# The key-value blocks of linear attention as four 32-column matmuls each instead of one 128-column matmul

## The chip, the cores and the metric

The kernel runs on one core of a Trainium2 chip. The metric is the device time of one execution in microseconds (us), taken as the median over several runs; one further execution is profiled, and every row shown here comes from that one.

## What is computed

The reference normalises x, runs linear attention over it, and multiplies the result with a gated feed-forward layer. The part that matters here is the state of the attention, `kv`: 32 heads, each with a 32x32 matrix.

```python
H = 32; Dh = D // H                      # D = 1024, S = 2048
phi = lambda t: jnp.where(t > 0, t + 1, jnp.exp(t)) + 1e-6
pq, pk = phi(q), phi(k)
kv = jnp.einsum("bhsd,bhse->bhde", pk, v)    # 32x32 for each head
z = jnp.einsum("bhsd->bhd", pk)
num = jnp.einsum("bhqd,bhde->bhqe", pq, kv)
den = jnp.einsum("bhqd,bhd->bhq", pq, z)[..., None] + 1e-6
...
xn = _layernorm(x, axis=-1)
s = A(xn)                                # (num / den) @ wo
g = _silu((_silu(xn @ w1) * (xn @ w3)) @ w2)
return x + s * g
```

## The kernel before

All large products are written as seven-product schemes on 2x2 blocks (names such as `B11`, `T2`, `S1`, `c22` are their operands and sums). Each single product is done by `mm3`: three matmuls of 128x512 on rounded high and low parts (lines 103, 104, 105). The order in which TensorE gets its work is the order in which the program is written; a scheduler places the instructions of the other engines.

The sequence tokens are handled in two halves. The second half projects keys and queries, then forms g, the product of the transposed normalised rows with the keys (`row_products`, `g_d`), so that kv can be had from g and the value columns of `wqkv` without forming v. After that the loop over 14 column pairs of w1 and w3 runs (`gemm`, names `ag`, `bg`, `cg`, `dg` for the gate and `au`, `bu`, `cu`, `du` for the up projection), and the rest of the attention is fed into it as small jobs: after each of the seven products, `catch_up` takes the next step of a queue of jobs (`attention_work`, `go_on`).

Two jobs matter here. `key_values(j)` makes the state of four heads (128 columns of D): its two steps, e = 0 and 1, each load a tile `gw` (four 128x128 blocks of g and four of the value weights) and accumulate four matmuls into one 128x128 part of a PSUM bank `kv`. There are eight j, so 16 steps in all, which I call kv blocks. These matmuls have plain float32 operands, and the trace shows two weight loads and two matmuls for each of them. Off the four 32x32 squares of the diagonal the 128x128 result mixes different heads, so after e = 1 VectorE multiplies it with `hmask` (one on the four squares, zero elsewhere) and writes `kvf`. `merge_wo` splits `kvf` into `kvm` and multiplies it with rows of wo (`wos`), giving `wp`.

Two older places in the kernel already put 32-column matmuls at separate column positions: `spread_z` (line 816, tile `zc`: eight matmuls of 128x32 weights with two columns streamed) and `denominators` (line 852, tile `den`: four matmuls at a time, 256 columns streamed).

Of the kernel before, what the change touches and what calls it, by code (L numbers as in the profile page):

```python
# [16 lines left out]
P = 128  # L17
# [5 lines left out]
def tile_linear_attention_times_swiglu(  # L23
# [10 lines left out]
    nc = tc.nc  # L34
# [3 lines left out]
    ND = D // P  # L38
# [5 lines left out]
    DH = D // H  # L44
# [6 lines left out]
    def bank(name):  # L51
        return ps.tile([P, C], F32, tag="bank", name=name)
# [5 lines left out]
    hmask = const.tile([P, P], F32, name="hmask")  # L58
# [64 lines left out]
    def job_tile(shape, name):  # L123
        return praw.tile(shape, F32, tag="job", bufs=4, name=name)
# [771 lines left out]
    kvf = {}  # L896

    def key_values(j):

        acc = []  # L900

        def load(e):
            t = job_tile([P, 2, ND // 2, P], f"gw{j}_{e}")
            nc.sync.dma_start(out=t[:, 0], in_=g_d[2 * e + j % 2][:, :, j // 2 * P:(j // 2 + 1) * P])
            rows = wqkv[e * C:(e + 1) * C, 2 * D + j * P:2 * D + (j + 1) * P]
            nc.sync.dma_start(out=t[:, 1], in_=rows.rearrange("(k p) n -> p k n", p=P))
            return t

        def steps(e, t):
            if not acc:  # L910
                acc.append(bank(f"kv{j}")[:, :P])
            for k in range(ND // 2):
                nc.tensor.matmul(acc[0], lhsT=t[:, 1, k], rhs=t[:, 0, k], start=e + k == 0, stop=bool(e) and k == ND // 2 - 1)
            if e:
                kvf[j] = st.tile([P, P], F32, tag="kvf", bufs=1, name=f"kvf{j}")
                nc.vector.tensor_mul(kvf[j], acc[0], hmask)
            yield True

        return [Job(lambda e=e: load(e), lambda t, e=e: steps(e, t)) for e in range(2)]
# [237 lines left out]
    def second_weights(i, n, k):  # L1157
        if (i, n, k) not in asked:
            ask(i, n, k, small)
        return asked[i, n, k]  # L1160
# [109 lines left out]
    def layer_place(n, i, k):  # L1270
        return (pw[0] if k else pw0).tile([P, 2, C], FR, tag=f"{n}_{k}", name=f"{n}_{k}")

    acc = []
    layers = [Segment(f"B{i}", (f1 - f0) // 2, i == 0, i == len(FB) - 1, layer_place,
                      lambda n, _, k, i=i: second_weights(i, n, k),
# [41 lines left out]
```

## Time and profile before

| | |
|---|---|
| median of 3 runs | 2343.28 us (2342.56 to 2346.6) |
| the profiled execution | 2346.91 us, of which the span is 2345.1 us |
| TensorE matmul busy | 2300.3 us, 98% of the span |
| VectorE, ScalarE, GpSimd busy | 1780.5, 923.9, 687.0 us |
| granted TensorE clock | 0.995 of full speed |
| kv matmuls (line 913) | 128 records of 274 ns mean, between 1162 and 1342 us |

In the views of the profile PE is TensorE's matmul side and PEld its weight load; DVE is VectorE, ACT ScalarE, POOL GpSimd. Matmuls are pipelined, so that a record lasts longer than the step from one start to the next. A timeline row with "x8" merges eight records: its length goes from the first start to the last end.

### The profile page before, as it was taken

Reading aid. Unit: us, or ns where it says so; the run is one execution under the profiler, and the core shown is the slowest. Engines: PE = TensorE matmul, PEld = TensorE weight load, DVE = VectorE, ACT = ScalarE, POOL = GpSimd, SP = SyncE. Lnnn points to the kernel's source line nnn. Section 1 sums busy time; section 2 is a strip of 40 time slices with the busy share of each in tenths; the row PEclk is TensorE's granted clock in tenths of the full one; section 3 lists DMA queues with packets and bytes.
Section 4 is the critical chain, followed back from the end, with each engine's and each line's share of the span. In section 5 each row is a group of like instructions: output and inputs, shape, how many; then the busy total and the mean of one; then the engine's idle time right before and its main releaser. Section 6 shows DMA issues by size and latency. Waiting matters only on the chain.

```text
span 2345.1 us, 30980 instructions
## 1 busy us (share of the span) xinstructions
PE 2300.3 (98%) x10368; PEld 1888.9 (81%) x10368; DVE 1780.5 (76%) x2830; ACT 923.9 (39%) x1639; POOL 687.0 (29%) x854
## 2 busy tenths in 40 slices
PE   6999999999999999999999999999999999999998
PEld 5788878888887888777888888888887888888876
DVE  8887888888877776557867688887755666767798
ACT  5555343433232554433243332334323634242433
POOL 5220333376766221001423434342310000000033
PEclk9999999999999999999999999999999999999999
DMA  6555455576668645786666666665756565665688
GB/s 234 179 184 179 153 184 184 169 227 215 215 218 314 224 146 191 257 257 204 211 188 187 193 195 216 195 217 166 242 173 193 171 191 178 219 211 182 189 267 265
DMA packets 353695, 479.69 MB, mean 205 GB/s; under 512 B 24208, under 2 KB 262800, under 8 KB 353424
## 3 DMA queue, kind: packets, MB, share of 16 engines
q1 hardware_dynamic: 315808, 357.63, 48.5%
q0 software_dynamic: 37728, 120.09, 15.8%
q8 instruction: 81, 1.33, 0.2%
q14 instruction: 78, 0.64, 0.1%
HBM read 306.71 MB, written 174.59 MB: 205 GB/s over the span
## 4 chain that ended last, share of the span: by engine, by line
PE 70%; DVE 5%; DMA 3%; issue 1%; ACT 1%; SPq 0%; DVEq 0%; ACTq 0%
PE g L103 2%; PE g L104 2%; PE g L105 2%; PE aB L105 1%; PE dB L103 1%; PE aB L103 1%; PE aB L104 1%; PE cB L105 1%; PE dB L104 1%; PE dB L105 1%; PE cB L104 1%; PE cB L103 1%; DMA rS4B<-h_d 1%; PE bB L103 1%; PE bB L104 1%
## 5 line engine op out<-in xcount | busy, mean ns | idle before, releaser
L751 POOL DMA_DIRECT2D h_d<-sg x112 | 82.8, 740 | 253.8 <-DVE sg L747 163.1
L1065 POOL DMA_DIRECT2D u_d<-uB x32 | 17.3, 541 | 403.4 <-DVE uB L1048 361.0
L96 DVE TENSOR_TENSOR xy<-xy,xy 128x512 fp32r<-128x512 f32 x112 | 73.0, 686 | 65.3 <-ACT xy L95 65.2
L95 ACT CAST xy<-xy 128x512 fp32r<-128x512 f32 x112 | 65.1, 620 | 102.5 <-PE g L105 56.8
L104 PE MATMUL g<-xy,xy 128*128 128x512 f32 x224 | 87.7, 391 | 1.0 <-DVE xy L96 1.0
L105 PE MATMUL g<-xy,xy 128*128 128x512 f32 x224 | 87.1, 390 | 0.0
L103 PE MATMUL g<-xy,xy 128*128 128x512 f32 x224 | 82.6, 398 | 0.0
L518 POOL DMA_DIRECT2D y_d<-y x48 | 34.6, 722 | 139.7 <-ACT y L538 79.8
L1048 DVE TENSOR_TENSOR acc<-cB,acc 128x512 f32<-128x512 f32 x50 | 34.4, 687 | 41.2 <-PE cB L105 41.2
L1048 DVE TENSOR_TENSOR acc<-dB,acc 128x512 f32<-128x512 f32 x56 | 38.5, 688 | 30.0 <-PE dB L105 29.8
L731 POOL TENSOR_TENSOR hs<-hs,sg 128x256 f32<-128x256 f32 x56 | 60.6, 1082 | 0.1
L733 POOL TENSOR_TENSOR hs<-sg 128x256 f32<-128x256 f32 x56 | 56.8, 1014 | 0.0
L103 PEld LDWEIGHTS g<-xy,xy 128*128 128x128 f32 x224 | 41.8, 187 | 14.1 <-issue 3.7
L889 POOL DMA_DIRECT2D qs_d<-qd x32 | 18.1, 565 | 117.4 <-DVE qd L885 80.1
L1179 POOL DMA_DIRECT2D s_d<-s x32 | 17.3, 541 | 117.6 <-DVE s L1048 69.7
L104 PEld LDWEIGHTS g<-xy,xy 128*128 128x128 f32 x224 | 42.1, 188 | 10.8 <-DVE xy L96 1.7
L734 POOL TENSOR_TENSOR hs<-sg,hs 128x256 f32<-128x256 f32 x56 | 49.9, 891 | 1.5
L730 POOL TENSOR_TENSOR hs<-sg,sg 128x256 f32<-128x256 f32 x56 | 50.0, 893 | 1.2
L766 POOL TENSOR_TENSOR w<-w 128x256 f32<-128x256 f32 x28 | 27.3, 975 | 78.5 <-DMA w<-in_B_w 78.3
L105 PEld LDWEIGHTS g<-xy,xy 128*128 128x128 f32 x224 | 42.1, 188 | 8.9
L759 POOL DMA_DIRECT2D h_d<-hs x60 | 45.8, 765 | 3.5 <-POOL hs L734 2.4
L95 ACT CAST XS4B<-rS4B 128x384 fp32r<-128x384 f32 (+1 forms) x40 | 19.7, 493 | 60.8 <-PE cB L105 41.1
(5315 smaller groups left out, 8316.8 us busy)
## 6 DMA issues: line engine op xcount, KB each, us to landing
h_d<-hs POOLq DMA_DIRECT2D x60, 256.0 KB, 3.5
h_d<-sg POOLq DMA_DIRECT2D x56, 256.0 KB, 3.8
w<-in_B_w SPq DMA_DIRECT2D x56, 256.0 KB
wt_d<-w SPq DMA_DIRECT2D x28, 512.0 KB
xy<-x_d SPq DMA_DIRECT2D x28, 512.0 KB
xy<-y_d SPq DMA_DIRECT2D x28, 512.0 KB
h_d<-hs SPq DMA_DIRECT2D x52, 256.0 KB
y_d<-y POOLq DMA_DIRECT2D x48, 256.0 KB, 3.0
```

Of the source, the lines that this page charges most:

```text
L95: nc.scalar.copy(out=hi, in_=src)
L96: return nc.vector.tensor_sub(out=lo, in0=src, in1=hi.bitcast(F32))
L103: nc.tensor.matmul(acc, lhsT=wh, rhs=ah, start=start, stop=False, skip_group_check=True)
L104: nc.tensor.matmul(acc, lhsT=wh, rhs=al, start=False, stop=False, skip_group_check=True)
L105: return nc.tensor.matmul(acc, lhsT=wl, rhs=ah, start=False, stop=stop, skip_group_check=True)
L730: e.tensor_add(out=s1, in0=a21, in1=a22)
L731: e.tensor_sub(out=s2, in0=s1, in1=a11)
L733: e.tensor_sub(out=s3, in0=a11, in1=a21)
L734: e.tensor_sub(out=s4, in0=a12, in1=s2)
L751: nc.gpsimd.dma_start(out=h_d[i][2 * h + c][:, 2 * n:4 * n + 2, k], in_=src)
L759: queue.dma_start(out=h_d[i][2 * h + c][:, 6 + 4 * e:10 + 4 * e, k], in_=o[e].rearrange("p (e s) -> p e s", s=P))
L1048: return V.tensor_add(out=c, in0=src, in1=c)
```

## The change

Each float32 matmul of 128x128 in `key_values` becomes four: for each of the four heads g the 128x32 slice of the value weights is the stationary operand on columns 32g to 32g+31 of TensorE, the matching 128x32 slice of g is streamed, and the 32x32 result goes to partitions 32g to 32g+31 of the PSUM tile, which is now 32 columns wide. So 256 matmuls stand where 64 stood. The multiplication with the mask reads the 32 columns four times, by a broadcast, and writes the same 128x128 `kvf`.

```diff
         def steps(e, t):
             if not acc:
-                acc.append(bank(f"kv{j}")[:, :P])
+                acc.append(bank(f"kv{j}")[:, :DH])
             for k in range(ND // 2):
-                nc.tensor.matmul(acc[0], lhsT=t[:, 1, k], rhs=t[:, 0, k], start=e + k == 0, stop=bool(e) and k == ND // 2 - 1)
+                for g in range(P // DH):
+                    c = slice(g * DH, (g + 1) * DH)
+                    nc.tensor.matmul(acc[0][c], lhsT=t[:, 1, k, c], rhs=t[:, 0, k, c], skip_group_check=True,
+                                     start=e + k == 0, stop=bool(e) and k == ND // 2 - 1, tile_position=(0, g * DH))
             if e:
                 kvf[j] = st.tile([P, P], F32, tag="kvf", bufs=1, name=f"kvf{j}")
-                nc.vector.tensor_mul(kvf[j], acc[0], hmask)
+                heads = [P, P // DH, DH]
+                nc.vector.tensor_mul(kvf[j].rearrange("p (g c) -> p g c", c=DH),
+                                     acc[0].unsqueeze(1).to_broadcast(heads), hmask.rearrange("p (g c) -> p g c", c=DH))
             yield True
```

On TensorE, at the first kv block, between the first product of a gate projection (`ag`) and its second (`bg`), the order before is:

```order
L104 MATMUL ag_2__9770<-A_1_6432,B11g_2__9702 128x512
L105 MATMUL ag_2__9770<-A_1_6432,B11g_2__9702 128x512
L913 MATMUL kv_9789<-gw_0_9618 128x128 x4
L103 MATMUL bg_2__9794<-S_1_6433,T2g_2__9766 128x512
L104 MATMUL bg_2__9794<-S_1_6433,T2g_2__9766 128x512
```

and after it (the numbers at the ends of names are counters and shift with the added instructions):

```order
L104 MATMUL ag_2__9770<-A_1_6432,B11g_2__9702 128x512
L105 MATMUL ag_2__9770<-A_1_6432,B11g_2__9702 128x512
L915 MATMUL kv_9789<-gw_0_9618 32x32 x16
L103 MATMUL bg_2__9806<-S_1_6433,T2g_2__9766 128x512
L104 MATMUL bg_2__9806<-S_1_6433,T2g_2__9766 128x512
```

Sixteen matmuls stand where four stood, at the same place; this is so at all 16 kv blocks, and nothing else moves on TensorE.

On VectorE, after the second kv block, where the mask is applied (`kvf`), `B11u` is an operand of the next up projection. Before:

```order
L464 TENSOR_TENSOR ug_2__9769<-bg_2__9794,ug_2__9769 128x512
L96 TENSOR_TENSOR B11u_2__9886<-wu_2__9700,B11u_2__9886 128x512
L916 TENSOR_TENSOR kvf_9820<-kv_9789,hmask 128x128
L347 TENSOR_TENSOR wu_2__9700<-wu_2__9700 128x4x128 x2
L471 TENSOR_TENSOR c22g_2__9834<-cg_2__9795,ug_2__9769 128x512
L96 TENSOR_TENSOR kvm_9843<-kvf_9820,kvm_9843 128x128
```

and after:

```order
L464 TENSOR_TENSOR ug_2__9769<-bg_2__9806,ug_2__9769 128x512
L920 TENSOR_TENSOR kvf_9844<-kv_9789,hmask 128x128
L96 TENSOR_TENSOR B11u_2__9910<-wu_2__9700,B11u_2__9910 128x512
L347 TENSOR_TENSOR wu_2__9700<-wu_2__9700 128x4x128 x2
L471 TENSOR_TENSOR c22g_2__9858<-cg_2__9807,ug_2__9769 128x512
L96 TENSOR_TENSOR kvm_9867<-kvf_9844,kvm_9867 128x128
```

The mask moves ahead of one neighbour. Such moves, by one or two places, are found at seven of the eight masks, and at two of them `kvm` moves ahead of a subtraction of line 347 as well. Besides, one subtraction of GpSimd (line 734) and one DMA issue of SyncE (line 759) move by a few places; ScalarE's order is the same.

## The prediction

> **What bounds the kernel now.** I read the page first, then the busy time by stages, then the chain of waits in the stage of the kv blocks, and last the timeline around single blocks.
>
> ```profile
> span 2345.1 us, 30980 instructions
> PE 2300.3 (98%) x10368; PEld 1888.9 (81%) x10368; DVE 1780.5 (76%) x2830; ACT 923.9 (39%) x1639; POOL 687.0 (29%) x854
> ```
>
> TensorE is busy for 98% of the span. Whether it is the bound in the stage of the change, and afterwards, is seen in the stretches from 1156 us (just before the first kv block) to 1345 us (just after the last), and from there to the end:
>
> ```profile
> 1156.00:1345.00 189.00, 189.00 (x897) 158.40 (x896) 133.29 (x188) 66.93 (x122) 68.59 (x74) 1.00 0.61 189
> 1345.00:1640.00 295.00, 295.00 (x1302) 244.19 (x1302) 244.70 (x409) 101.99 (x173) 114.67 (x136) 1.00 0.64 199
> 1640.00:2345.00 705.00, 691.51 (x3036) 568.39 (x3034) 493.18 (x837) 266.73 (x514) 84.62 (x119) 1.00 0.67 207
> ```
>
> The first number is the length, the second PE's busy time, the fourth DVE's (133 of 189 us in the first row), the one after the counts the granted clock. In the first two stretches PE has no gap at all; in the last it lacks 13.5 of 705 us. So what is taken from PE between 1156 and 1345 us should come off the end, unless something that PE nearly waits for becomes late. The chain of waits in the window from 1150 to 1350 us agrees:
>
> ```profile
> by line: PE kv L913 7.1%; PE wp L103 1.6%; PE wp L105 1.6%; PE wp L104 1.6%; PE du__10685 L104 0.9%; PE du__10685 L105 0.9%; PE cu__11035 L103 0.9%; PE du__10685 L103 0.9%; PE dg__10872 L105 0.9%; PE cg__9795 L103 0.9%; PE cu__9966 L103 0.9
> 1162.45 0.89 PE kv L913 x8
> ...
> 1175.14 0.23 PE wp L103
> ...
> 1341.13 0.89 PE kv L913 x8
> ```
>
> All of it is PE work, and the kv blocks are 7.1% of 200 us, 14.2 us, in sixteen pieces of 0.89 us. This is the most that the change could ever win: 0.6% of the time.
>
> **The change part by part.** What a block costs now is read around the first one, on PE:
>
> ```profile
> 1161.61 0.39 PE L103 MATMUL ag__9770<-A,B11g__9702 128*128 128x512 f32 x1
> 1161.83 0.39 PE L104 MATMUL ag__9770<-A,B11g__9702 128*128 128x512 f32 x1
> 1162.06 0.39 PE L105 MATMUL ag__9770<-A,B11g__9702 128*128 128x512 f32 x1
> 1162.29 1.05 PE L913 MATMUL kv<-gw 128*128 128x128 f32 x8
> 1163.10 0.48 PE L103 MATMUL bg__9794<-S,T2g__9766 128*128 128x512 f32 x1
> 1163.41 0.40 PE L104 MATMUL bg__9794<-S,T2g__9766 128*128 128x512 f32 x1
> ```
>
> Without a block, a 512-column matmul starts 0.227 us after the one before (1161.61, 1161.83, 1162.06). From 1162.06 to 1163.41 there are 1.35 us with two such steps in them, 0.45 us, so the block costs 0.90 us; it is the same for all 16, since the chain shows 0.89 at the first and the last. Inside it the eight records (two for each of the four float32 matmuls) step by (1.05 - 0.275)/8 = 0.10 to 0.11 us, 0.275 us being the length of one.
>
> The new block is not in this trace, but its form is. Tile `zc` has matmuls of plain float32 with 128x32 weights on rotating column positions, like the new ones, only with two columns streamed instead of 32, and eight matmuls (16 records) instead of 16 (32 records). Around it:
>
> ```profile
> 924.34 0.22 PEld L816 LDWEIGHTS zc<-eps,zb 128*32 128x32 f32 x16 [0.35 <-issue]
> ...
> 924.03 0.39 PE L105 MATMUL g<-xy,xy 128*128 128x512 f32 x1
> 924.35 0.31 PE L816 MATMUL zc<-eps,zb 128*32 128x2 f32 x16
> 924.58 0.50 PE L103 MATMUL g<-xy,xy 128*128 128x512 f32 x1
> 924.92 0.40 PE L104 MATMUL g<-xy,xy 128*128 128x512 f32 x1
> 925.15 0.39 PE L105 MATMUL g<-xy,xy 128*128 128x512 f32 x1
> ```
>
> Three things are to be seen. The weight loads do not start under the matmul before, as they do in the old block, but after 0.35 us in which the profile shows nothing to wait for: entering the 32-column form costs a drain, and leaving it another, as the 0.34 us step after 924.58 shows. Still, from 924.03 to 924.92 are only 0.89 us, 0.44 us above two normal steps. And the 16 records run four at a time. The timeline cut off later and later in this block shows how it grows:
>
> ```profile
> 924.35 0.21 PE L816 MATMUL zc<-eps,zb 128*32 128x2 f32 x4
> ...
> 924.35 0.24 PE L816 MATMUL zc<-eps,zb 128*32 128x2 f32 x8
> ...
> 924.35 0.28 PE L816 MATMUL zc<-eps,zb 128*32 128x2 f32 x12
> ```
>
> Each further group of four, one for each column position, adds 0.03 us (0.21, 0.24, 0.28, 0.31). Does streaming more columns break this? Tile `den` streams 256 at each of the four positions:
>
> ```profile
> 926.53 0.39 PE L105 MATMUL g<-xy,xy 128*128 128x512 f32 x1
> 926.85 0.64 PE L852 MATMUL den<-pqd,zb 128*32 128x256 f32 x8
> 927.41 0.50 PE L103 MATMUL g<-xy,xy 128*128 128x512 f32 x1
> 927.75 0.39 PE L104 MATMUL g<-xy,xy 128*128 128x512 f32 x1
> ...
> 926.85 0.42 PE L852 MATMUL den<-pqd,zb 128*32 128x256 f32 x4
> ```
>
> The second group of four adds 0.64 - 0.42 = 0.22 us, so a column costs about 0.22/256 = 0.86 ns for all four positions together, and 32 columns 27 ns. That is just under the 0.03 us step of `zc`, which must then be set by the loading of 32 weight columns, and loading and streaming overlap (the old block shows it too: loads and matmuls of 0.19 and 0.275 us in steps of 0.11). So I take 0.032 us for each group of four, that is for both streaming and loading.
>
> The new block has 32 records, eight groups of four. Its cost is that of `zc`, 0.45 us (0.44 by the step at 924.92, a few hundredths more by the slower steps just behind), plus four more groups at 0.032, 0.13 us, plus 0.03 us for the 30 columns by which its last group streams longer: 0.61 us. The check with `den`: two groups fewer than `zc`, -0.06, and 254 more columns in each of two, +0.43 less the 0.03 that the load had cost, gives 0.79; measured from 926.53 to 927.75 it is 0.77. So the block goes from 0.90 to 0.61 us, and 16 of them save 16 x 0.29 = 4.7 us (4.2 to 5.2 for 0.02 us of uncertainty in each block and the read-off).
>
> VectorE's mask now reads 32 PSUM columns four times:
>
> ```profile
> 1166.81 0.69 DVE L96 TENSOR_TENSOR B11u__9886<-wu__9700,B11u__9886 128x512 fp32r<-128x512 f32 x1
> ...
> L916 DVE TENSOR_TENSOR kvf<-kv,hmask x8: 282/283/292, 1167.4 to 1342.5; 128x128 f32<-128x128 f32 x8
> L96 DVE TENSOR_TENSOR kvm<-kvf,kvm x8: 281/283/293, 1170.3 to 1345.4; 128x128 fp32r<-128x128 f32 x8
> ```
>
> It makes as many elements, so I take the same 283 ns; a broadcast read could at worst double it, 2.3 us over all eight. Either way it is hidden: DVE is free for 56 of the 189 us, and from the first `kvf` (1167.4 us) on `kvm` comes at 1170.3 and `wp` on PE only at 1175.14 us (in the chain above). The moves of this mask by one or two neighbours, of 283 ns against 0.69 us, have the same cover; without it PE would wait by at most that, 0.7 us at a block. Loads, their sizes and their issue places are unchanged. The new matmuls' only waits are those for the loads at the head of each block, as before.
>
> What is late next? Nothing in the stage, where PE has no gap at all; later PE waits 13.5 us in total, which a 4.7 us earlier arrival could lengthen a little. I take nothing off for it. The profiled execution of 2346.91 us (2345.1 span) would be 2342.2; against the median of 2343.28 us the forecast is **2338.6 us**. The change is 0.20%, and 0.2% (4.7 us) is about what a measurement of this kernel can tell from no change, so the forecast lies on the edge between faster and the same.
>
> **The rivals.** *The groups of four run one after another.* `zc` streams two columns, and its weights are loaded once for each position; in the new block each position has other streamed data. If every record took its own 0.032 us, the 32 of them would take 1.02 us where I count 0.26, the block 1.37, and the time would rise by 16 x 0.47 = 7.5 us to **2350.8**. Against it stands `den`, where four positions with other data each stream 256 columns in the time of one. The Trainium skill, "TensorE: Matmul & The Clock Gate", section "Wait — 56ns, not 53.3ns?", says that matmuls never start closer than about 25 ns to each other however few columns they stream. By that 32 records would take 0.8 us and the time would rise by about 4 us, an estimate from that page; the trace disagrees, since the 16 records of `zc`, of 0.17 us each, lie within 0.31 us, 9 ns apart. I give 0.11 to this rival.
>
> *TensorE's sequencer cannot feed the blocks*, the rival that ends slower by most. How far it runs ahead is seen from its waits for the loads:
>
> ```profile
> L913 PEld LDWEIGHTS kv<-gw x128: 187/192/192, 1162.1 to 1341.6; 128*128 128x128 f32 x128
> L913 PEldq EVENT_SEMAPHORE  x16: 51/51/51, 1158.2 to 1337.6; - x16
> ```
>
> The first wait passes at 1158.2, 3.9 us before the first load starts: 17 steps of 0.227 us, about 34 instructions. `zc` has 32 in all, so it may have stood in that queue as a whole; the new block has 64, of which some 30 must come while it runs. The old block proves only 0.055 us for each (a load and a matmul in 0.11). At that the 30 need 1.65 us, the block costs 2.0 us, and the time rises by 16 x 1.1 = 17.6 us to **2361**. It decides from 18 ns an instruction on, where the block is back at 0.90 us. The same page and section give 62 ns for a matmul whenever the sequencer decodes in software, which by my estimate from it would make the time rise by about 7 us. One place in the trace speaks against both, at the start of the kernel, in the window from 36.85 to 37.1 us and the timeline behind it:
>
> ```profile
> L165 PEldq EVENT_SEMAPHORE  x2: 51/51/51, 36.9 to 37.0; - x2
> ...
> 37.35 0.60 PE L165 MATMUL tS<-ident,xb 128*128 128x128 f32 x4
> 37.79 0.60 PE L165 MATMUL tS<-ident,S1x 128*128 128x128 f32 x4
> 38.23 0.60 PE L165 MATMUL tA<-ident,xb 128*128 128x128 f32 x4
> 38.66 0.33 PE L165 MATMUL tS<-ident,xa 128*128 128x128 f32 x1
> ```
>
> Of these groups of transposes the first and the last need two engines each, and so a wait of the sequencer's own. Between the two waits it issued the first three groups, 24 instructions, in less than 0.15 us: 6 ns each or less. I give this rival 0.08.
>
> *What is gained in the stage is lost behind it.* The longest of PE's waits after 1345 us is this:
>
> ```profile
> PE cB L103 <- DVE acc L1048: 1.0, 1, 1.0
> ```
>
> VectorE is not hurried by an earlier PE, and the DMA engines are busy for 67% of the last stretch; were the whole gain to end in such a wait, the time would stay at **2343.3**. Against it: the longest wait is 1.0 us and came once, and 1345 to 1640 us has none. I give it 0.13.
>
> **How the numbers follow.** My forecast has 0.68. Of that, 0.47 goes to a gain over 0.2% and 0.21 to one just below, since its own range of 2337 to 2340.5 us (4.2 to 5.2 us saved, and the scatter of medians) is cut in the middle, and a stretch that is all PE leaves little that could eat into it. With the lost gain the chance of "same" is 0.34; the two rivals that slow it down hold 0.19. The range of 2336.5 to 2346 us takes in the forecast and the lost gain, up to near the highest of the runs shown (2346.6), and leaves out the two slower rivals.
>
> **What would show it.** In the changed profile PE should have 512 records of the new kv line instead of 128, so 10752 in all; a block should show the idle time of some 0.35 us before its first load, its 32 records should lie within 0.46 us (0.26 from first to last start), and the step from the 512-column matmul before it to the second one behind should be 1.06 instead of 1.35 us. From 1156 us to the end of the last block it should take 4.7 us less, without PE waiting for `kvf`, `kvm` or `wos`. The mask should stay near 283 ns. Records of a block spread evenly over 1 us mean that the positions run in turn; a burst of half of them and then a trickle means the sequencer; blocks as forecast with longer waits after 1640 us mean the lost gain.

## The result and the profile after

The changed kernel takes 2338.3 us (median of 15 runs, 2336.32 to 2342.83), the one before in the same comparison 2344.15 us; the ratio is 0.9979, with a 95% interval from 0.9972 to 0.9986. That is 5.85 us or 0.2% less: a small gain, but the interval lies wholly below 1. The forecast was 2338.6 us. The profiled execution took 2340.79 us.

The page of the changed kernel, PE's stretches from before the first block to behind the last and from 1635 us to the end (length, then PE's busy time), and the chain of waits from 1150 to 1350 us:

```profile
span 2339.0 us, 31747 instructions
PE 2296.4 (98%) x10752; PEld 1880.5 (80%) x10752; DVE 1778.8 (76%) x2830; ACT 926.3 (40%) x1639; POOL 691.1 (30%) x854
...
1155.50:1345.50 190.00, 190.00 (x1306) 153.10 (x1306) 138.67 (x196) 69.27 (x126) 68.89 (x73) 1.00 0.65 197
...
1635.00:2339.00 704.00, 691.06 (x3035) 568.38 (x3033) 492.37 (x836) 267.29 (x514) 85.93 (x119) 1.00 0.67 207
...
1161.84 0.39 PE kv L915 x32
1162.22 0.43 PE bg__9806 L103
...
1336.12 0.39 PE kv L915 x32
```

PE is as full as before. A kv block is 0.39 us in the chain where it was 0.89, but the matmul behind it has 0.43 us in the chain where a normal step is 0.23, so part of the price of leaving the 32-column form is counted there. So I compare from the first to the last block: 1162.45 to 1341.13 is 178.68 us before, 1161.84 to 1336.12 is 174.28 us now. Fifteen blocks lie between, and 4.40/15 = 0.293 us each, 4.7 us for sixteen. The spans differ by 6.1 us; the other 1.4 us are spread over the time before 1160 us (0.6 us, where the two programs are the same) and after the stage (0.8 us), which I take for the scatter of single executions.

The first block in the timeline of PE, with the weight loads first, and the same block cut off at two earlier points:

```profile
1161.76 0.35 PEld L915 LDWEIGHTS kv<-gw 128*32 128x32 f32 x32 [0.35 <-issue]
...
1161.45 0.39 PE L105 MATMUL ag__9770<-A,B11g__9702 128*128 128x512 f32 x1
1161.77 0.46 PE L915 MATMUL kv<-gw 128*32 128x32 f32 x32
1162.15 0.50 PE L103 MATMUL bg__9806<-S,T2g__9766 128*128 128x512 f32 x1
1162.49 0.39 PE L104 MATMUL bg__9806<-S,T2g__9766 128*128 128x512 f32 x1
...
1161.77 0.24 PE L915 MATMUL kv<-gw 128*32 128x32 f32 x4
1161.77 0.36 PE L915 MATMUL kv<-gw 128*32 128x32 f32 x19
```

Before its first load the weight-load side stands idle for 0.35 us, for which the profile names no releaser. The 32 records lie within 0.46 us, and from 1161.45 to 1162.49 are 1.04 us, 0.59 above two normal steps.

### The profile page after: what moved, and what is told of

It reads as the page before. It is cut to its first block, busy times and chain, and to the rows that moved or that the text cites. A ratio compares the mean times of both kernels' runs of the same rounds, so it can differ in the third digit from the quotient of the medians.

```text
span 2339.0 us, 31747 instructions
## 1 busy us (share of the span) xinstructions
PE 2296.4 (98%) x10752; PEld 1880.5 (80%) x10752; DVE 1778.8 (76%) x2830; ACT 926.3 (40%) x1639; POOL 691.1 (30%) x854
## 4 chain that ended last, share of the span: by engine, by line
PE 69%; DVE 6%; issue 5%; DMA 5%; ACT 1%; POOL 0%; SPq 0%; DVEq 0%; ACTq 0%; POOLq 0%
PE g L103 2%; PE g L104 2%; PE g L105 2%; PE cB L103 1%; PE cB L105 1%; PE cB L104 1%; PE dB L105 1%; PE dB L103 1%; PE dB L104 1%; PE aB L105 1%; PE aB L103 1%; PE aB L104 1%; PE bB L105 1%; PE bB L103 1%; PE bB L104 1%
```

## The experiments

The theory is the one of the forecast: a block costs about 0.33 us for entering and leaving the 32-column form and some 0.032 us for every group of four records, one at each column position. Below, the cost of a block is read as before, from the last 512-column matmul ahead of it to the second behind it, less two steps of 0.227 us. Experiments with one run are read from their traces alone, since single times scatter by several us. The diffs show the lines that matter, against the changed kernel.

### The change again, twice

No edit; two more comparisons of the changed kernel.

> The changed kernel once more, beside the next three on one chip. The theory (a kv block costs 0.61 us instead of 0.90 us, sixteen times, all of it on TensorE and none given back): 4.7 us below the kernel before, ratio 0.998. The rival that the 6 us of the first comparison hold another gain besides the blocks: 6 us or more below again.

> The changed kernel a third time, on another chip, to narrow its ratio: 4.7 us from the blocks less what a stray wait takes, 0.998 to 0.9985.

Measured: ratios 0.9988 (0.9979 to 0.9997) and 0.9980 (0.9972 to 0.9989), medians 2339.37 against 2343.18 us and 2339.5 against 2343.4 us, so 3.8 and 3.9 us less than before. Both profiled executions show one wait of PE in the stage, the same in both, which the profile of the kernel before and the first one of the changed kernel do not have:

```profile
PE dg__10607 L103 <- DVE c22g__10641 L477: 0.6, 1, 0.6
```

The blocks cost what they cost in the first profile. In these executions 0.6 of the 4.7 us is given back, because VectorE has not yet read the PSUM bank that the next product writes (line 477). Of the VectorE operations ahead of it, the one on `T1u` (line 96) took 1.78 us in both, against 0.68 us in the first profile of the changed kernel; why is open. In the profile of the kernel before it took 1.78 us too, without a wait of PE. Both comparisons come out below 4.7 us, which speaks against another gain besides the blocks. Their intervals reach from 0.7 to 4.9 and from 2.6 to 6.6 us, so the first of the two excludes a gain of 6 us and the second alone would not.

### All 128 columns streamed at each position, with the old mask

```diff
-                acc.append(bank(f"kv{j}")[:, :DH])
+                acc.append(bank(f"kv{j}")[:, :P])
...
-                    nc.tensor.matmul(acc[0][c], lhsT=t[:, 1, k, c], rhs=t[:, 0, k, c], skip_group_check=True,
+                    nc.tensor.matmul(acc[0][c], lhsT=t[:, 1, k, c], rhs=t[:, 0, k], skip_group_check=True,
...
+                nc.vector.tensor_mul(kvf[j], acc[0], hmask)
```

> Still 32 weight columns at four positions, but each position streams all 128 columns of g, and the mask is the old one over 128x128. Theory (the gain comes from streaming a quarter of the columns at each position, side by side): each group of four takes 0.11 us instead of 0.033, first to last start of a block 0.80 instead of 0.26 us, the block costs 1.23 us; 10 us above the changed kernel and 5 us above the one before. Rival one (the gain comes from the mask reading 32 columns, or from the moved VectorE order): as slow as before, 0.0 to 0.5 us off. Rival two (it comes from four positions as such): as fast as the changed kernel.

Measured: 2351.04 us, ratio 1.0034 (1.0021 to 1.0047), 7.9 us above the kernel before. The first block on PE:

```profile
1161.54 0.39 PE L105 MATMUL ag__9770<-A,B11g__9702 128*128 128x512 f32 x1
1161.86 1.08 PE L915 MATMUL kv<-gw 128*32 128x128 f32 x32
1162.87 0.50 PE L103 MATMUL bg__9806<-S,T2g__9766 128*128 128x512 f32 x1
1163.21 0.40 PE L104 MATMUL bg__9806<-S,T2g__9766 128*128 128x512 f32 x1
```

From 1161.54 to 1163.21 are 1.67 us, 1.22 above two steps; I had expected 1.23. The 0.32 us more than in the old block make 5.1 us for sixteen, which is also what the spans of the two profiled executions differ by (2350.2 against 2345.1 us); the 7.9 us of the medians have an interval from 4.9 to 11.0 us. So neither rival fits: the time is not that of the kernel before, nor that of the changed one. Four positions as such are a loss here, since eight groups at 0.11 us take as long as the eight records of the old block and the drain comes on top. The gain of the change is that each position streams a quarter of the columns while the other three do the same.

### Both steps in one block, in the new form and in the old

The first tile is kept at e = 0, and all matmuls are issued at e = 1:

```diff
-            for k in range(ND // 2):
-                for g in range(P // DH):
-                    c = slice(g * DH, (g + 1) * DH)
-                    nc.tensor.matmul(acc[0][c], lhsT=t[:, 1, k, c], rhs=t[:, 0, k, c], skip_group_check=True,
...
             if e:
+                for i in range(ND):
+                    k = i % (ND // 2)
+                    for g in range(P // DH):
+                        c = slice(g * DH, (g + 1) * DH)
+                        u = both[i // (ND // 2)]
+                        nc.tensor.matmul(acc[0][c], lhsT=u[:, 1, k, c], rhs=u[:, 0, k, c], skip_group_check=True,
+                                         start=i == 0, stop=i == ND - 1, tile_position=(0, g * DH))
```

> Both steps of a column group in one block: nothing is done at e = 0, and at e = 1 all eight pieces of the contraction, 64 matmuls, 128 records. Theory (of the 0.61 us of a block 0.35 are entering and leaving the 32-column form, 0.033 a group): eight entries fewer, 16 groups in each block, 0.88 us for it instead of twice 0.61, 2.7 us below the changed kernel. Rival (TensorE's sequencer can feed only what stands in its queue of some 33 instructions; 64 went well because half of them stood there): the second half of a block comes slower than 0.033 us a group, and the gain shrinks or turns. Rival two (the first tile is held longer, the loads behind it come late): a wait of TensorE for gw.

> The version with both steps in one block again, beside the changed kernel. Theory: eight drains of 0.33 us fewer, 2.6 us below the changed kernel, ratio to the kernel before 0.9969 to 0.9975. Rival (its lead over the changed kernel was scatter): within 1 us of it.

The control does the same to the kernel before: `nc.tensor.matmul(acc[0], lhsT=u[:, 1, k], rhs=u[:, 0, k], start=i == 0, stop=i == ND - 1)` over all eight i at e = 1, with the old mask.

> The control for the one with 64 matmuls in a block: the kernel before, with both steps in one block of eight 128x128 matmuls. Theory (the old form has no drain at its entry, and at its exit only some 0.1 us): 0.1 us less for each pair, 0.8 us in total, the same as before within the interval. Rival (putting the steps together is itself the gain, by fewer interruptions of the projections): 2 us or more below the kernel before.

Measured in the new form: 2335.63 and 2337.25 us, ratios 0.9972 (0.9963 to 0.9982) and 0.9969 (0.9958 to 0.9980), so 3.7 and 2.3 us below the changed kernel beside it. In the old form: 2343.7 us, ratio 1.0003 (0.9995 to 1.0012). The block of the new form, and of the old:

```profile
1165.86 0.39 PE L105 MATMUL bg__9789<-S,T2g__9766 128*128 128x512 f32 x1
1166.18 0.76 PE L920 MATMUL kv<-gw 128*32 128x32 f32 x64
1166.87 0.51 PE L103 MATMUL cg__9790<-S,T3g__9731 128*128 128x512 f32 x1
1167.21 0.39 PE L104 MATMUL cg__9790<-S,T3g__9731 128*128 128x512 f32 x1
```

```profile
1161.72 0.39 PE L105 MATMUL bg__9789<-S,T2g__9766 128*128 128x512 f32 x1
1161.95 1.95 PE L917 MATMUL kv<-gw 128*128 128x128 f32 x16
1163.65 0.48 PE L103 MATMUL cg__9790<-S,T3g__9731 128*128 128x512 f32 x1
1163.96 0.40 PE L104 MATMUL cg__9790<-S,T3g__9731 128*128 128x512 f32 x1
```

In the new form the joint block costs 1.35 - 0.45 = 0.90 us where two of the changed kernel cost 1.2; in the old form it costs 1.79 us, as much as two of 0.90. Joining steps is worth something only where a block has a switch of form to save. The saving of 0.3 us for each pair is close to the third of a microsecond that I take for the price of switching; the next experiment shows what the difference is. The old form lost not even the 0.1 us that I had expected of it. PE never waits for `gw` although the first tile is held longer. In the second profile of the joint form PE waits 0.9 us at the place where the changed kernel waited 0.6. This version is faster than the kernel before in both comparisons. Against the changed kernel the intervals of the ratios overlap in both, so its lead there rests on the blocks: 0.3 us less for each of eight pairs, 2.4 us.

### The same matmuls twice

```diff
-            for k in range(ND // 2):
+            for i in range(ND):
+                k = i % (ND // 2)
```

> Each block does its 16 matmuls twice over (kv is doubled by it; the work is what counts). Theory: eight more groups of four at 0.033 us, a block at 0.88 us instead of 0.61, 4.2 us above the changed kernel, just below the kernel before; first to last start 0.53 us. Rival (the feed of TensorE's queue): the groups beyond the queue come slower, above 0.6 us from first to last start.

Measured (kv comes out doubled; the time alone is of interest): 2343.35 us, ratio 1.0001 (0.9992 to 1.0011). The first block, and cut off earlier and earlier:

```profile
1160.75 0.39 PE L105 MATMUL ag__9770<-A,B11g__9702 128*128 128x512 f32 x1
1161.07 0.76 PE L916 MATMUL kv<-gw 128*32 128x32 f32 x64
1161.76 0.51 PE L103 MATMUL bg__9822<-S,T2g__9766 128*128 128x512 f32 x1
1162.10 0.39 PE L104 MATMUL bg__9822<-S,T2g__9766 128*128 128x512 f32 x1
...
1161.07 0.61 PE L916 MATMUL kv<-gw 128*32 128x32 f32 x48
1161.07 0.52 PE L916 MATMUL kv<-gw 128*32 128x32 f32 x36
1161.07 0.46 PE L916 MATMUL kv<-gw 128*32 128x32 f32 x32
```

A block costs 0.90 us, 0.02 more than expected. The first eight groups end at 0.46 us, 0.03 us apart; the ninth ends 0.06 us later, the next three 0.03 us apart, and the last four take 0.15 us together. So the second half is some 0.05 us longer than eight steps of 0.03 us, and the joint block of the experiment before has the same length (0.76 us for 64 records): without this loss, joining two blocks would have saved the third of a microsecond. A feed as slow as the forecast's rival needs is excluded: the rival decides from 18 ns an instruction on, and beyond the 34 or so instructions that stand ready, over 90 more came in about 0.57 us, 6 ns each at most. What causes the loss in the second half stays open; that a feed of some 4 ns an instruction has a part in it is not excluded.

### Two heads at a time on 64 columns

```diff
-                for g in range(P // DH):
-                    c = slice(g * DH, (g + 1) * DH)
+                for g in range(2):
+                    c = slice(g * 2 * DH, (g + 1) * 2 * DH)
```

> Two heads at a time: 64 weight columns at two positions, 64 columns streamed, the mask reading 64 columns twice. Theory (steps go with the columns loaded and streamed): eight groups of two at 0.058 us, 0.43 us from first to last start, a block at about 0.82 us. Rival (the drain at entry and exit is longer or shorter with the number of positions): the same steps, but another fixed part than 0.35 us.

One run, 2342.64 us. The first block:

```profile
1160.70 0.39 PE L105 MATMUL ag__9770<-A,B11g__9702 128*128 128x512 f32 x1
1161.02 0.69 PE L915 MATMUL kv<-gw 128*64 128x64 f32 x16
1161.63 0.50 PE L103 MATMUL bg__9798<-S,T2g__9766 128*128 128x512 f32 x1
1161.96 0.39 PE L104 MATMUL bg__9798<-S,T2g__9766 128*128 128x512 f32 x1
```

1.26 - 0.45 = 0.81 us, as expected (0.82). The entry (0.32 us from the matmul before to the first record) is the same with two positions of 64 columns as with four of 32, and the step goes with the columns.

### Head by head, and two pieces of a head at a time

The order of the same 16 matmuls in a block:

```diff
-            for k in range(ND // 2):
-                for g in range(P // DH):
+            for g in range(P // DH):
+                for k in range(ND // 2):
```

> The same 16 matmuls of a block, head by head: the four pieces of the contraction for head 0, then for head 1 and so on, so that neighbours in the order share a column position. Theory (the hardware takes instructions out of order from a queue of some 33, so 16 instructions of one head and 16 of the next are seen at a time): two positions run side by side, 16 steps of 0.033 us, 0.5 us from first to last start, a block at 0.85 us. Rival one (it runs in the order written): 32 steps of 0.032, 1.0 us, a block at 1.4 us. Rival two (each position has its own queue, filled far ahead): 0.26 us and 0.61 us as in the changed kernel.

and, between the two, `for g, k in [(g, k + k0) for k0 in (0, 2) for g in range(P // DH) for k in range(2)]`.

> The 16 matmuls of a block in the order: two pieces of the contraction for head 0, two for head 1, 2 and 3, then the other two pieces in the same way. Head by head, each head's first weight load came just after the sixth of the eight loads of the head before, and the block took 0.70 us from first to last start. Theory (a position can hold two records, a load and its matmul each, that wait for their turn, while the queue goes on to the next position; a third blocks it): with four records a visit the next head starts after the second load of the one before, some 0.03 us; 0.3 to 0.35 us from first to last start, a block at 0.65 to 0.70 us. Rival (only two positions ever run side by side unless neighbours in the order alternate): half of 32 steps of 0.032, 0.5 us, a block at 0.85 us.

Each has one run, 2345.86 and 2346.5 us. The first blocks, head by head and then with two pieces:

```profile
1158.98 0.39 PE L105 MATMUL ag__9770<-A,B11g__9702 128*128 128x512 f32 x1
1159.30 0.90 PE L915 MATMUL kv<-gw 128*32 128x32 f32 x32
...
1160.46 0.39 PE L104 MATMUL bg__9806<-S,T2g__9766 128*128 128x512 f32 x1
```

```profile
1163.12 0.39 PE L105 MATMUL ag__9770<-A,B11g__9702 128*128 128x512 f32 x1
1163.44 0.49 PE L915 MATMUL kv<-gw 128*32 128x32 f32 x32
...
1164.20 0.39 PE L104 MATMUL bg__9806<-S,T2g__9766 128*128 128x512 f32 x1
```

Head by head a block costs 1.48 - 0.45 = 1.03 us, more than the 0.85 I had expected and more than the old block: the change would have been a loss in this order. The loads of one head are about 30 ns apart in the trace; 2 to 3 ns behind the sixth of eight comes another one, which I take for the first of the next head, so positions overlap only at the seam. With two pieces a visit the block costs 0.63 us, a little under the 0.65 to 0.70 that I had expected and close to the changed kernel. That two positions at most run side by side is excluded by it. But the idea that a position holds two waiting pairs of load and matmul, and that a third holds up all that is behind it, does not fit either: the next head's first load comes some 0.013 us after that of the head before, sooner than the 0.03 us I had named and before the second of that head's four loads (0.028 us), when three pairs still wait. So a limit exists, as eight records in a row show, but its depth stays open.

## Why the prediction was right

The bound was read rightly: PE has no gap in the stage, so what a block saves comes off the time. The cost of the new block, built from `zc` and `den`, was 0.61 us against 0.59 measured by the same reading (for the step that the prediction named, 1.06 us forecast and 1.04 measured), and 0.293 us saved per block, taken from the first block to the last, is the 0.29 of the sum. Its terms hold one by one: the entry (0.35 us idle without a releaser), the step of a group (0.24 to 0.46 us for the seven groups behind the first, 0.031 each), the step set by columns (64 and 128 columns streamed), the fixed part (joint blocks, with the loss in their second half). One slip has no weight: from the first to the last start of the old block's eight records there are seven steps, not eight, so they are 0.11 us, the upper of the two figures given.

That the time came within 0.3 us of the forecast is luck. The forecast stood on a median of 2343.28 us of three runs; over fifteen it is 2344.15, and the gain was 5.85 us, 1.15 us more than the sum. The two later comparisons gave 3.8 and 3.9 us, 0.8 to 0.9 less than the sum. What holds without luck is the cost of a block, which is read from the traces.

The mask's time did not change although it now reads by a broadcast, and PE waits neither for `kvf` nor for `kvm` in the stage:

```profile
L920 DVE TENSOR_TENSOR kvf<-kv,hmask x8: 280/281/285, 1165.8 to 1336.8; 128x128 f32<-128x128 f32 x8
```

Wrong was the sentence that nothing is late next in the stage: VectorE is, by 0.6 us at one place, in two of the three profiles of the changed kernel. It may be part of why the later comparisons came out at 3.8 and 3.9 us; the scatter of the medians is as large, so this isn't shown.

Of the rivals, groups that run one after another are excluded, as the traces have four records for each 0.03 us. The Trainium skill, "TensorE: Matmul & The Clock Gate", section "Wait — 56ns, not 53.3ns?", states about 25 ns as the least time between the starts of two matmuls; across column positions these traces do not bear that out. The starved queue is excluded: the changed kernel's block of 64 instructions runs through at 0.03 us a group, and the doubled block of 128 bounds the feed at 6 ns an instruction. The same section of the Trainium skill gives 62 ns for a matmul when the sequencer decodes it in software; the 64 matmul records of a doubled block, which start within 0.57 us, show that this is not the case here. The gain lost behind the stage did not come: from 1635 us to the end PE lacks 12.9 of 704 us, where before it lacked 13.5 of 705.

## What to carry to other kernels

A new form of instruction can be priced before it runs if the trace holds the same form at another size: here one tile gave the entry, the exit and the step of a group, another the price of a column, and the sum was right to 0.02 us. Here splitting a matmul over column positions paid only where the streamed columns shrank with it, each visit cost a third of a microsecond for the switch, and the order must not stay on one position for long: two matmuls in a row did little harm, four made the change a loss. So it is worth gathering such blocks: by the traces, joining two brought about half of the change's own gain once more.

## What the runs showed of the hardware that I had not expected

The order of instructions decides whether column positions overlap: 0.26 us from first to last start when the heads alternate, 0.30 with two pieces a visit, 0.70 head by head, for the same 32 records. And entering and leaving the split form costs about a third of a microsecond with two positions of 64 columns as with four of 32, while the old full-width block of plain float32 shows no such price at its entry: its first record starts 0.23 us after the 512-column matmul before it, a normal step, where that of a split block starts after 0.32.
